# Issuing the attention scores inside the output matmuls, and re-splitting the fill's evacuations, in a fused attention and FFN kernel

## The chip, the cores and the metric

The kernel runs on one core of a Trainium2 chip. The metric is the device time of one execution in microseconds (us). A profiled execution also gives a span, which is about 1.8 us less than the time measured for the same execution. The granted clock is the share of TensorE's full speed that the profile reports; a drop is a stretch in which it reads 0.50.

## The reference, cut to what matters

For each of 64 heads (8 batches, 8 heads, 576 tokens, 64 channels) the reference adds two attentions: one over a band of 7 tokens, and one over the sequence pooled 4 to 1. The result, 4608 tokens of 512 channels, goes through a gated FFN.

```python
out_d     = softmax(scale * q_d @ k_d.T) @ v_d           # pooled 4:1, then repeated 4 times
out_local = softmax(where(|i-j| < 4, scale * q @ k.T, -1e9)) @ v
x   = (out_up + out_local)                               # [4608, 512]
out = (relu(x @ w_gate) * (x @ w_val)) @ w_out           # d_ff = 1536
```

## The kernel before: the parts that matter

The kernel handles two heads ("a pair", `hp`) at a time. The first four pairs are done alone (the fill). Then 36 slots follow; a slot does a quarter of an FFN chunk of 512 tokens (three `h` groups of 8 matmuls, one `y` group of 12) and, up to slot 27, one pair of attention. The program is scheduled by hand: each engine gets its instructions in the order in which they are written. `ps` is the program's result buffer in PSUM, eight banks of 128x512 values. Every matmul writes into a bank, and ScalarE or VectorE has to read a result out (an evacuation) before the program writes that bank again. A dummy is a matmul on zeros, put in to keep TensorE's clock up.

```python
def emit_qkT_pe(hp, b0, b1):                # fill and slots 0 to 3: transpose and pool q, k on TensorE
    ...                                     # 24 matmuls into three PSUM banks
    nc.scalar.copy(out=big[:, 0], in_=t0[:, :, 0:96])            # bank 1 of 3
    nc.scalar.copy(out=sml[:, 0], in_=t0[:, :, 96:120])
    nc.vector.tensor_copy(out=sml[:, 1:3], in_=t1[:, :, :, 96:120])   # banks 2 and 3
    nc.vector.tensor_copy(out=big[:, 1:3], in_=t1[:, :, :, 0:96])

def emit_s1(hp, p0):                        # scores: four banks p0..p0+3, then exp and mask
    for c in range(2):                      # c=0 writes p0, p0+1; c=1 writes p0+2, p0+3
        ...
def emit_s2w(hp):                           # weighted sum into banks 4 to 7
    ...
    # ScalarE: Ln, Ln, Exp ; VectorE: two multiplies, banks 4-5 then 6-7, which frees them
def emit_fill(hp):
    emit_in(hp + 4); emit_s1(hp, 2); emit_vd(hp, 6)
    emit_warm(3)                            # dummy matmuls 128x512 on zeros
    if hp >= 1: emit_x_pe(hp - 1, 0)        # x back to channels-first; ScalarE copies it out
    if hp < LEAD - 1: emit_qkT_pe(hp + 1, 2, 3)
    else: emit_warm(3)
    emit_s2(hp, 6, 0); emit_warm(1)

def emit_slot(s, gate):                     # cut: slots above 4
    ...
    if s > 4:
        if hp < NP: emit_s1(hp, 4)          # scores in banks 4 to 7
        emit_y(c - 1, s % 4, 2)             # 12 matmuls
        ...                                 # slots 5 to 8: emit_vd
        if hp + 1 < NP: emit_pool(hp + 1)   # VectorE: reduce for the next pair's pooled scores
        emit_h(c, jj, 0)()
        if hp < NP: emit_s2w(hp)
        emit_h(c, jj + 1, 1)()
        gate = emit_h(c, jj + 2, 0)
        ...
    # slots 1 to 4: other order; slot 4 issues emit_pool(9) after its scores
...
emit_warm(15)                               # before the first pair
```

The softmax here doesn't subtract the row's maximum and nothing guards it: scores larger than these inputs give would overflow.

Of the kernel before, what the change touches and what calls it, by code (L numbers as in the profile page):

```python
# [12 lines left out]
ALU = mybir.AluOpType  # L13
# [33 lines left out]
def _sap(t_ap: bass.AP, part, extra_off: int, free_dims) -> bass.AP:  # L47
    pitch = t_ap.ap[0][0]
    lo, n = part
    return bass.AP(  # L50
        tensor=t_ap.tensor,
        offset=t_ap.offset + lo * pitch + extra_off,
        ap=[[pitch, n]] + list(free_dims),
    )
# [3 lines left out]
def kernel(  # L58
# [10 lines left out]
    nc = tc.nc  # L69
# [14 lines left out]
    NTP = 9  # L84
# [122 lines left out]
    def emit_qkT_pe(hp, b0, b1):  # L207
        r, r4, r2 = hp % NL, hp % 4, hp % 2
        sv = qk16[r].rearrange("p i (h j d) -> p i h j d", h=2, d=64)
        for n in range(2 * NB):  # L210
            lo = 120 * (n % 4)
            bank = b0 if n < 4 else b1 + n // 4 - 1
            for hh in range(2):
                nc.tensor.matmul(  # L214
                    out=ps[64 * hh : 64 * hh + 64, bank, lo : lo + 120],
                    lhsT=sv[:, n // NB, hh, n % NB, :],
                    rhs=eyesum_sb,
                    start=True,
                    stop=True,
                )  # L220
        big = qkT[r4][:, 0 : 2 * S].rearrange("p (b n t) -> p b n t", b=3, n=4)
        sml = qkd[r2].rearrange("p i t -> p (i t)").rearrange("p (b n t) -> p b n t", b=3, n=4)
        t0 = ps[:, b0, 0:480].rearrange("p (n t) -> p n t", n=4)
        t1 = ps[:, b1 : b1 + 2, 0:480].rearrange("p b (n t) -> p b n t", n=4)
        nc.scalar.copy(out=big[:, 0], in_=t0[:, :, 0:96])
        nc.scalar.copy(out=sml[:, 0], in_=t0[:, :, 96:120])
        nc.vector.tensor_copy(out=sml[:, 1:3], in_=t1[:, :, :, 96:120])
        nc.vector.tensor_copy(out=big[:, 1:3], in_=t1[:, :, :, 0:96])

    def emit_vd_pool(hp):  # L230
        t, m, o = v4[hp % NV4], v2[hp % 2], vd[hp % 3]
# [65 lines left out]
    def emit_s2(hp, bank, pu):  # L297
        r2 = hp % 2
        x = xo[hp % 3]
        vflat = vw[hp % NL].rearrange("p b c -> p (b c)")  # L300
        for hh in range(2):
            for tcx in range(2):
                for c in range(2):
                    s0 = c * SD + 72 * tcx
                    lo = 130 * hh + 65 * tcx
                    nc.tensor.matmul(
                        out=ps[:, bank, lo : lo + 65],
                        lhsT=ed[r2][:, hh, s0 : s0 + 128],
                        rhs=vd[hp % 3][:, c, 127 * hh : 127 * hh + 65],
                        start=(c == 0),  # L310
                        stop=(c == 1),
                    )
        for hh in range(2):
            for j in range(NB):
                nc.tensor.matmul(
                    out=ps[:, 2 * pu + hh, 65 * j : 65 * j + 65],
                    lhsT=ee[r2][:, hh, NQ * j : NQ * j + 128],
                    rhs=vflat[:, 128 * (NB * hh + j) - hh : 128 * (NB * hh + j) - hh + 65],
                    start=True,
                    stop=True,  # L320
                )
        rd = small.tile([72, 2, 2], FP32, name="rd", tag="rd")
        nc.vector.reciprocal(out=rd, in_=_sap(ps, (0, 72), 512 * bank + 64, [[66, 2], [65, 2]]))
        nc.vector.tensor_tensor(
            out=x[0:72, NB : NB + 2, :].rearrange("p t (h d) -> p h t d", h=2),
            in0=_sap(ps, (0, 72), 512 * bank, [[131, 2], [65, 2], [1, 64]]),
            in1=_sap(rd, (0, 72), 0, [[2, 2], [1, 2], [0, 64]]),
            op=ALU.mult,
        )
        ru = small.tile([96, 2, NB], FP32, name="ru", tag="ru")  # L330
        nc.vector.reciprocal(out=ru, in_=_sap(ps, (0, 96), 1024 * pu + 64, [[448, 2], [65, NB]]))
        nc.vector.tensor_tensor(
            out=x[:, 0:NB, :].rearrange("p j (h d) -> p h j d", h=2),
            in0=_sap(ps, (0, 96), 1024 * pu, [[513, 2], [65, NB], [1, 64]]),
            in1=_sap(ru, (0, 96), 0, [[NB, 2], [1, NB], [0, 64]]),
            op=ALU.mult,
        )

    def emit_s2t(hp, between):
        r2 = hp % 2  # L340
# [95 lines left out]
    def emit_x_pe(hp, pp):  # L436
        b, kk = hp // NPB, hp % NPB
        x = xo[hp % 3]
        for g in range(2):
            flat = pair(pp)[:, g, 0:288]  # L440
            nc.tensor.matmul(
                out=flat, lhsT=x[0:72, NB + g, :], rhs=rep4_sb, start=True, stop=False
            )
            for jj in range(3):
                nc.tensor.matmul(
                    out=flat[:, NQ * jj : NQ * jj + NQ],
                    lhsT=x[:, 3 * g + jj, :],
                    rhs=eye_sb,
                    start=False,
                    stop=(jj == 2),  # L450
                )
        o = xT[:, kk, b * S : b * S + S].rearrange("p (g t) -> p g t", g=2)
        nc.scalar.copy(out=o, in_=pair(pp)[:, :, 0:288])

    gts = {}

# [18 lines left out]

        return gate

    def emit_y(c, ty, bank):
        y_ps = ps[:, bank, :]
        for jj in range(NJJ):  # L480
            nc.tensor.matmul(  # L481
                out=y_ps,
                lhsT=gts[c, jj][:, bass.ts(ty, 128)],
                rhs=wo_sb[:, jj, :],
                start=(jj == 0),
                stop=(jj == NJJ - 1),
            )
        y_sb = ffn.tile([128, D_MODEL], FP32, name="y_sb", tag="y_sb")
        nc.scalar.copy(out=y_sb, in_=y_ps)  # L489
        r0 = c * TCH + ty * 128  # L490
        done = 0
        while done < 128:
            real = (r0 + done + B0 * S) % NTOK
            n = min(128 - done, NTOK - real)
            nc.scalar.dma_start(
                _dap(out, real * D_MODEL, [[D_MODEL, n], [1, D_MODEL]]), y_sb[done : done + n, :]
            )
            done += n
# [32 lines left out]
    def emit_fill(hp):  # L531
        emit_in(hp + 4)
        emit_s1(hp, 2)
        emit_vd(hp, 6)
        emit_warm(3)
        if hp >= 1:
            emit_x_pe(hp - 1, 0)
        if hp < LEAD - 1:
            emit_qkT_pe(hp + 1, 2, 3)
        else:  # L540
            emit_warm(3)
        emit_s2(hp, 6, 0)
        emit_warm(1)

    def emit_slot(s, gate):
        c, jj, hp = s // 4, 3 * (s % 4), s + LEAD
        if NVP <= hp + 1 < NP:
            emit_vd_pool(hp + 1)
        emit_in(hp + 4)
        if NTP <= hp + 3 < NP:  # L550
            emit_qkT(hp + 3)
        if s == 0:
            emit_qkT_pe(hp, 2, 3)
            emit_warm(2)
            emit_x_pe(hp - 1, 0)
            emit_warm(1)
        elif s <= 5:
            emit_s2t(hp - 1, gate)
        elif gate:
            gate()  # L560
        if s > 4:
            if hp < NP:
                emit_s1(hp, 4)
            emit_y(c - 1, s % 4, 2)
            if hp < NVP:
                emit_vd(hp, 3)
            if hp + 1 < NP:
                emit_pool(hp + 1)
            emit_h(c, jj, 0)()
            if hp < NP:  # L570
                emit_s2w(hp)
            emit_h(c, jj + 1, 1)()
            gate = emit_h(c, jj + 2, 0)
            if hp < NP:
                gate()
                emit_xsum(hp)
                return None
            return gate
        if s == 4:
            emit_y(c - 1, s % 4, 1)  # L580
        else:
            emit_h(c, jj, 0)()
        emit_s1(hp, 4)
        if NTP <= hp + 1:
            emit_pool(hp + 1)
        if s == 4:
            emit_h(c, jj, 0)()
        emit_h(c, jj + 1, 1)()
        emit_vd(hp, 5)
        if hp + 1 < NTP:  # L590
            emit_qkT_pe(hp + 1, 4, 0)
        return emit_h(c, jj + 2, 3)

    with tc.manual_schedule(engines={ET.PE, ET.DVE, ET.Activation, ET.SP, ET.Pool}):
        nc.sync.dma_start(cst_sb, cst_dr)
        for hp in range(4):
            emit_in(hp)
        emit_warm(15)
        emit_qkT_pe(0, 2, 3)
        for hp in range(LEAD):  # L600
            emit_fill(hp)
        gate = None
        for s in range(NCH * 4):
            gate = emit_slot(s, gate)
        gate()
        for ty in range(4):
            emit_y(NCH - 1, ty, ty)
# [30 lines left out]
```

## Time and profile before

| | before |
|---|---|
| time, median of the three runs given | 373.0 us (373.0 to 374.79) |
| span of the profiled execution (time 374.69) | 372.8 us |
| TensorE busy | 96% of the span |
| steady slot, slots 9 to 27 (slots 6 to 8, with emit_vd, take 9.89) | 9.55 us |
| one pair of the fill | 4.47 us |

The page's first part gives each engine's busy time, its share of the span and its instructions; PEld is the weight load.

```profile
span 372.8 us, 7223 instructions
PE 357.8 (96%) x2871; PEld 181.1 (49%) x2871; DVE 228.9 (61%) x332; ACT 211.5 (57%) x355; POOL 177.9 (48%) x219
```

The 96% does not say that TensorE is the limit. The chain of waits does better: it lists, in order of time, what the end of the program hung on. Start, duration and engine of one steady slot of the kernel before (the query lists the longest pieces; the weighted sum, before Ln, and the scores, before y, are left out):

```profile
135.05 2.70 PE ps L481 x12
137.74 1.73 PE ps L461 x8
139.90 0.77 ACT rden_113 L423
140.69 0.77 ACT rden_113 L423
141.48 0.81 ACT rden_113 L426
142.36 0.89 issue
143.25 0.92 DVE xn_115 L429
144.60 2.70 PE ps L481 x12
```

L481 is y, L461 is h, L423 and L426 are Ln and Exp, L429 the multiply. "issue" covers the first of the two multiplies. The period is one loop through three engines, and for about 4 us of it, from Ln to the second multiply, TensorE does h work that is not on the loop. The timeline of the same slot shows where the loop touches TensorE (start, duration, engine, operation; in brackets the idle time before it and what ended that):

```profile
142.32 1.84 DVE L429 TENSOR_TENSOR xn_115<-ps,rden_113 64x720 f16<-64x720 f32 x2 [2.06 <-ACT rden_113 L426]
142.68 1.03 PE L461 MATMUL ps<-xT,wv_sb 128*128 128x512 f16 x4
143.64 0.25 PE L261 MATMUL ps<-qkd_100 64*72 64x144 f16 x2
144.22 0.25 PE L261 MATMUL ps<-qkd_100 64*72 64x144 f16 x2 [0.20 <-DVE xn_115 L429]
144.53 2.76 PE L481 MATMUL ps<-wo_sb,gT 128*128 128x512 f16 x12
```

The first half of the scores (L261 and its band part) starts at 143.64. The second half writes banks 6 and 7 and waits until the second multiply has read them, at 144.16. From the end of h, about 143.54, to y at 144.53 is 0.99 us; the same scores without a wait, in slot 0, took 0.59.

In the fill the same reading gives another engine. VectorE's copy of two banks ends last, and the next scores wait for it:

```profile
17.39 0.95 DVE L228 CAST qkT_98<-ps 128x768 f16<-128x768 f32 x1
18.39 0.22 PE L261 MATMUL ps<-qkd_100 64*72 64x144 f16 x1 [0.27 <-DVE qkT_98 L228]
```

Slot 5 is a place of its own. The table of stretches gives the stretch, its length, the busy time of PE, PEld, DVE, ACT and POOL with their instructions, the granted TensorE clock, and the DMA share and GB/s:

```profile
71.00:74.60 3.60, 2.00 (x49) 1.59 (x49) 1.59 (x2) 2.90 (x5) 3.60 (x5) 1.00 2.14 179
74.60:79.00 4.40, 4.36 (x14) 1.69 (x14) 2.76 (x4) 0.69 (x2) 3.05 (x5) 0.61 2.01 138
```

TensorE stood still several times before 74.6 us, and then its clock fell; y took 4.44 us there instead of 2.70.

### The profile page before, as it was taken

What the parts mean: (1) busy time and instruction counts of PE and PEld (TensorE: products, weight loads), DVE (VectorE), ACT (ScalarE), POOL (GpSimd) and SP (SyncE); (2) the same over time, 40 slices, a digit from 0 to 9 for tenths busy, and PEclk for the clock granted to TensorE, in tenths of its full rate; (3) what the DMA queues carried; (4) which work ended last, traced back from release to release, by engine and by line L of the source; (5) the groups of instructions that cost most, each with busy time, mean ns of one, the idle gap of its engine ahead of it and who ended that gap; (6) DMA issues with size and microseconds to landing.
All of it is one profiled execution on the core that took longest, in us unless ns stands there. A gap on an engine that the chain in (4) does not pass through costs nothing.

```text
span 372.8 us, 7223 instructions
## 1 busy us (share of the span) xinstructions
PE 357.8 (96%) x2871; PEld 181.1 (49%) x2871; DVE 228.9 (61%) x332; ACT 211.5 (57%) x355; POOL 177.9 (48%) x219
## 2 busy tenths in 40 slices
PE   7899999899999999999999999999999999999995
PEld 3665555445554444444444444444444544444442
DVE  8674566538777877777777667776666522222220
ACT  2664775646666666666666666666666533332321
POOL 8966548757667776777777777621000000000000
PEclk9999999989999999999999999999999999999999
DMA  9999999999999999999999999961000001000012
GB/s 129 169 173 184 177 196 124 169 134 175 180 107 115 118 132 113 132 123 111 127 128 122 125 122 125 120 100 48 28 31 28 30 28 56 31 28 30 28 56 84
DMA packets 165137, 39.51 MB, mean 106 GB/s; under 512 B 149264, under 2 KB 160368, under 8 KB 165104
## 3 DMA queue, kind: packets, MB, share of 16 engines
q0 software_dynamic: 132528, 22.48, 81.8%
q1 hardware_dynamic: 27376, 7.14, 15.0%
q10 hardware_dynamic: 5200, 9.44, 7.3%
q8 instruction: 22, 0.36, 0.4%
q14 instruction: 11, 0.09, 0.1%
HBM read 45.28 MB, written 9.44 MB: 147 GB/s over the span
## 4 chain that ended last, share of the span: by engine, by line
PE 65%; ACT 17%; DVE 10%; issue 7%; DVEq 0%
PE ps L461 29%; PE ps L481 26%; ACT rden_112 L423 5%; ACT rden_113 L423 5%; DVE xn_115 L429 3%; DVE xn_114 L429 3%; ACT rden_113 L426 2%; ACT rden_112 L426 2%; PE ps L261 2%; PE ps L405 2%; PE ps L214 1%; PE ps L245 1%; PE ps L272 1%; PE ps L413 1%; DVE xn_114 L383 1%
## 5 line engine op out<-in xcount | busy, mean ns | idle before, releaser
L461 PE MATMUL ps<-xT,wg_sb 128*128 128x512 f16 x432 | 111.0, 379 | 1.3 <-DVE xn_114 L383 0.5
L461 PE MATMUL ps<-xT,wv_sb 128*128 128x512 f16 x432 | 110.9, 379 | 0.0
L481 PE MATMUL ps<-wo_sb,gT 128*128 128x512 f16 x432 | 100.5, 384 | 0.6 <-DVE xn_114 L383 0.6
L461 PEld LDWEIGHTS <-wv_sb 128*128 128x128 f16 x432 | 42.3, 98 | 51.0
L481 PEld LDWEIGHTS <-gT 128*128 128x128 f16 x432 | 40.8, 99 | 48.9 <-issue 2.9
L461 PEld LDWEIGHTS <-wg_sb 128*128 128x128 f16 x432 | 39.7, 97 | 43.8 <-issue 1.5
L489 ACT COPY y_sb<-ps 128x512 f32<-128x512 f32 x36 | 21.1, 587 | 69.8 <-PE ps L481 69.8
L429 DVE TENSOR_TENSOR xn_115<-ps,rden_113 64x720 f16<-64x720 f32 x24 | 21.7, 905 | 24.7 <-ACT rden_113 L426 24.3
L429 DVE TENSOR_TENSOR xn_114<-ps,rden_112 64x720 f16<-64x720 f32 x22 | 19.9, 905 | 22.8 <-ACT rden_112 L426 22.4
L281 ACT ACTIVATE ee_102<-ps 112x576 f16<-112x576 f32 x32 | 19.5, 650 | 10.6 <-PE ps L272 10.0
L281 ACT ACTIVATE ee_103<-ps 112x576 f16<-112x576 f32 x32 | 19.5, 650 | 9.4 <-PE ps L272 9.2
L284 DVE TENSOR_TENSOR ee_102<-ee_102,cst_sb 112x576 f16<-112x576 f16 x32 | 21.1, 691 | 2.7 <-ACT ee_102 L281 2.5
L423 ACT ACTIVATE rden_113<-ps 64x720 f32<-64x720 f32 x24 | 18.4, 765 | 6.6 <-PE ps L413 6.3
L423 ACT ACTIVATE rden_112<-ps 64x720 f32<-64x720 f32 x22 | 16.8, 765 | 6.0 <-PE ps L413 5.8
L284 DVE TENSOR_TENSOR ee_103<-ee_103,cst_sb 112x576 f16<-112x576 f16 x32 | 19.8, 659 | 0.0
L527 PE MATMUL ps<-zero_sb 128*128 128x512 f16 x37 | 12.5, 463 | 1.3 <-DVE zero_sb L130 1.3
L261 PE MATMUL ps<-qkd_101 64*72 64x144 f16 x64 | 8.5, 244 | 3.8 <-DVE xn_114 L429 2.2
L261 PE MATMUL ps<-qkd_100 64*72 64x144 f16 x64 | 8.2, 245 | 3.8 <-DVE xn_115 L429 2.2
L388 DVE TENSOR_TENSOR xT<-xn_115 128x576 f16<-128x576 f16 x14 | 11.2, 798 | 0.1
L388 DVE TENSOR_TENSOR xT<-xn_114 128x576 f16<-128x576 f16 x14 | 10.5, 753 | 0.1
L290 ACT ACTIVATE ed_104<-ps 72x576 f16<-72x576 f32 x16 | 10.2, 639 | 0.0
L290 ACT ACTIVATE ed_105<-ps 72x576 f16<-72x576 f32 x16 | 10.2, 638 | 0.0
(457 smaller groups left out, 589.5 us busy)
## 6 DMA issues: line engine op xcount, KB each, us to landing
out_dram<-y_sb ACTq DMA_DIRECT2D x35, 256.0 KB, 3.3
wg_sb<-in_moe_w_gate_dram POOLq DMA_DIRECT2D x4, 384.0 KB, 10.0
wv_sb<-in_moe_w_val_dram POOLq DMA_DIRECT2D x4, 384.0 KB, 10.3
wo_sb<-in_moe_w_out_dram POOLq DMA_DIRECT2D x4, 384.0 KB, 11.7
vw_90<-in_v_dram POOLq DMA_DIRECT2D x5, 168.0 KB, 5.8
vw_91<-in_v_dram POOLq DMA_DIRECT2D x5, 168.0 KB, 5.4
vw_92<-in_v_dram POOLq DMA_DIRECT2D x5, 168.0 KB, 6.2
vw_89<-in_v_dram POOLq DMA_DIRECT2D x4, 168.0 KB, 8.0
```

The costliest lines, as they stand in the source:

```text
L261: nc.tensor.matmul(out=ps[0:72, p0 + 2 * c + hh, 288:432], lhsT=qkd[r2][lo : lo + 64, 1, bass.ts(c, 72)], rhs=qkd[r2][lo : lo + 64, 0, :], ...
L281: nc.scalar.activation(out=o, in_=ps[0:WK, p0 + 2 * g : p0 + 2 * g + 2, 0:288], func=AF.Exp, scale=scale)
L284: nc.vector.tensor_tensor(out=o, in0=o, in1=_sap(masks_sb, (0, WK), 288 * g, [[0, 2], [1, 288]]), op=ALU.mult,)
L290: nc.scalar.activation(out=ed[r2][:, :, 0 : 2 * SD].rearrange("p h (c t) -> p c h t", c=2), in_=ps[0:72, p0 : p0 + 4, 288:432].rearrange(" ...
L388: nc.vector.tensor_tensor(out=xT[:, kk, b * S : (b + 1) * S].rearrange("p (c t f) -> p c t f", c=2, f=4), in0=x[:, :, 0:288].rearrange("p ...
L423: nc.scalar.activation(out=r[lo : lo + 64], in_=ps[de : de + 64, 4 + 2 * hh : 6 + 2 * hh, 0:360], func=AF.Ln)
L426: nc.scalar.activation(out=r, in_=r, func=AF.Exp, scale=-1.0)
L429: nc.vector.tensor_tensor(out=x[lo : lo + 64], in0=ps[lo : lo + 64, 4 + 2 * hh : 6 + 2 * hh, 0:360], in1=r[lo : lo + 64], op=ALU.mult,)
L461: nc.tensor.matmul(out=h, lhsT=w[:, kk, bass.ts(jj, 128)], rhs=xT[:, kk, c * TCH : (c + 1) * TCH], start=(kk == 0), stop=(kk == 3),)
L481: nc.tensor.matmul(out=y_ps, lhsT=gts[c, jj][:, bass.ts(ty, 128)], rhs=wo_sb[:, jj, :], start=(jj == 0), stop=(jj == NJJ - 1),)
L489: nc.scalar.copy(out=y_sb, in_=y_ps)
L527: nc.tensor.matmul(out=ps[:, 7, :], lhsT=zero_sb[:, 0:128], rhs=zero_sb[:, 128:640], start=True, stop=True)
```

## The change

The intent is to keep TensorE working while the last multiply frees its banks. Scores are issued after two of y's matmuls; slot 5 has a form of its own. In the fill, two of the three banks go to ScalarE, the x copy goes to VectorE, the last pair's norm and copy are halved so that h can start earlier, and nine dummies are dropped. The pooling reduce for pair 9 moves from slot 4 to slot 5.

```diff
@@ emit_qkT_pe
-        nc.scalar.copy(out=big[:, 0], in_=t0[:, :, 0:96])
-        nc.scalar.copy(out=sml[:, 0], in_=t0[:, :, 96:120])
-        nc.vector.tensor_copy(out=sml[:, 1:3], in_=t1[:, :, :, 96:120])
-        nc.vector.tensor_copy(out=big[:, 1:3], in_=t1[:, :, :, 0:96])
+        for i, bank in enumerate((b0, b1, b1 + 1)):
+            t = ps[:, bank, 0:480].rearrange("p (n t) -> p n t", n=4)
+            if i < 2:
+                nc.scalar.copy(out=big[:, i], in_=t[:, :, 0:96])
+                nc.scalar.copy(out=sml[:, i], in_=t[:, :, 96:120])
+            else:
+                nc.vector.tensor_copy(out=sml[:, i], in_=t[:, :, 96:120])
+                nc.vector.tensor_copy(out=big[:, i], in_=t[:, :, 0:96])
@@ emit_s2: for the last pair of the fill the norm in two halves, (0,3) and (3,6)    ... (cut)
@@ emit_x_pe
-        nc.scalar.copy(out=o, in_=pair(pp)[:, :, 0:288])
+        if hp == LEAD - 1:
+            nc.scalar.copy(out=o[:, 0], in_=ps[:, 2 * pp, 0:288])
+            nc.vector.tensor_copy(out=o[:, 1], in_=ps[:, 2 * pp + 1, 0:288])
+        else:
+            nc.vector.tensor_copy(out=o, in_=pair(pp)[:, :, 0:288])
@@ emit_y
-    def emit_y(c, ty, bank):
+    def emit_y(c, ty, bank, cut=0, inner=None):
         for jj in range(NJJ):
+            if inner and jj == cut:
+                inner()
@@ emit_fill
-        emit_warm(3)
+        emit_warm(2)
@@ emit_slot
             emit_s2t(hp - 1, gate)
+            if s == 5:
+                emit_pool(hp)
...
             if hp < NP:
-                emit_s1(hp, 4)
-            emit_y(c - 1, s % 4, 2)
+                emit_y(c - 1, s % 4, 1 if s == 5 else 2, 6 if s == 5 else 2, lambda: emit_s1(hp, 4))
+            else:
+                emit_y(c - 1, s % 4, 2)
...
-        if NTP <= hp + 1:
-            emit_pool(hp + 1)
@@ start
-        emit_warm(15)
+        emit_warm(10)
```

More of the change, by code (lines that the diff above doesn't have):

```diff
@@ L222, in emit_qkT_pe @@
         sml = qkd[r2].rearrange("p i t -> p (i t)").rearrange("p (b n t) -> p b n t", b=3, n=4)
-        t0 = ps[:, b0, 0:480].rearrange("p (n t) -> p n t", n=4)
-        t1 = ps[:, b1 : b1 + 2, 0:480].rearrange("p b (n t) -> p b n t", n=4)
-        nc.scalar.copy(out=big[:, 0], in_=t0[:, :, 0:96])
-        nc.scalar.copy(out=sml[:, 0], in_=t0[:, :, 96:120])
-        nc.vector.tensor_copy(out=sml[:, 1:3], in_=t1[:, :, :, 96:120])
-        nc.vector.tensor_copy(out=big[:, 1:3], in_=t1[:, :, :, 0:96])
+        for i, bank in enumerate((b0, b1, b1 + 1)):
[6 more added lines that the diff above has]
+                nc.vector.tensor_copy(out=big[:, i], in_=t[:, :, 0:96])
     def emit_vd_pool(hp):
@@ L331, in emit_s2 @@
         nc.vector.reciprocal(out=ru, in_=_sap(ps, (0, 96), 1024 * pu + 64, [[448, 2], [65, NB]]))
-        nc.vector.tensor_tensor(
-            out=x[:, 0:NB, :].rearrange("p j (h d) -> p h j d", h=2),
-            in0=_sap(ps, (0, 96), 1024 * pu, [[513, 2], [65, NB], [1, 64]]),
-            in1=_sap(ru, (0, 96), 0, [[NB, 2], [1, NB], [0, 64]]),
-            op=ALU.mult,
-        )
+        for j0, j1 in ((0, 3), (3, 6)) if hp == LEAD - 1 else ((0, 6),):
+            nc.vector.tensor_tensor(
+                out=x[:, j0:j1, :].rearrange("p j (h d) -> p h j d", h=2),
+                in0=_sap(ps, (0, 96), 1024 * pu + 65 * j0, [[513, 2], [65, j1 - j0], [1, 64]]),
+                in1=_sap(ru, (0, 96), j0, [[NB, 2], [1, j1 - j0], [0, 64]]),
+                op=ALU.mult,
+            )
     def emit_s2t(hp, between):
```

## The prediction

> **What bounds it now.** TensorE is busy 96% of the span (busy table). From 296 us on (timeline) it has no wait and the change touches nothing. Before that:
>
> *Steady part, slots 6 to 27 (86 to 296 us).* A slot lasts 9.55 us (y, 12 matmuls of 128x512, starts at 144.53 and 154.08). The chain of waits runs Ln, Exp, two normalising multiplies on VectorE, second half of the scores, y, h, weighted sum. In the timeline the scores start at 143.64, their second half waits until 144.21 for the last multiply to free its banks, y starts at 144.53. From end of h (143.54) to y is 0.99 us; without the wait (slot 0, 31.14 to 31.73) the same scores cost 0.59. The stall is 0.40 us, in 22 slots (waits table: 11 + 11).
>
> *Fill (0 to 29.4 us).* A pair takes 4.47 us: scores, exp, pooled exp, transposing matmuls, evacuation; VectorE's 0.95 us copy of two banks ends last and holds the next scores (18.39).
>
> *Slot 5 (71 to 79 us).* TensorE waits several times, and the stretch table shows its clock at 0.61 from 74.6 to 79: y takes 4.44 instead of 2.70 us.
>
> **What the change does.**
>
> 1. *Scores after two y matmuls.* These take 0.43 us, so the second half would start 0.73 us after h ends; the multiply ends 0.64 after: just covered. TensorE's work per slot is then 2.59 (y) + 5.18 (h) + 0.78 (sum) + 0.59 (scores) = 9.14; the ScalarE-VectorE loop, shorter by 0.43, gives 9.12. I expect 9.15: 22 x 0.40 = **8.8 us gained**. VectorE idles 2.06 us per slot and does not take over.
>
> 2. *Fill.* VectorE keeps one bank (about 0.7 us instead of 1.25, estimated from its copies' time per element); ScalarE does two (2 x 0.62) and loses the 0.64 us x copy. ScalarE ends last; a pair takes about 4.05: three times 0.43. The first scores come 0.6 us earlier: VectorE's memsets end at 8.26 and only 0.7 follows. Halved norm and x copy before the first h: 0.3. Sum **2.1 us**. Fewer dummies save little themselves (k lands at 6.4) and may leave the clock low longer: the first run at 0.43 us each, and the Trainium skill ("TensorE: Matmul & The Clock Gate", Part 1) says about 3.4 us of sustained activity is needed for full rate. I take off 0.3.
>
> 3. *Slot 5.* y goes to another bank and six of its matmuls precede the scores. But the pooling reduce (1.35 us) that these scores need moves from slot 4, where VectorE had time, to behind the normalised sum (ends 75.38). Scores then start near 76.8, not 72.5; TensorE idles about 3.5 us, and the clock probably drops again. Scores and the other six end near 78.7 fast, 80 slow, against 78.9 before: **0.6 us lost**.
>
> **Sum.** 373.0 - 8.8 - 1.8 + 0.6 = **363.0 us**; range 360.5 to 366.0. Chances: faster 0.88, same 0.12, slower 0.0.
>
> **What would show it.** Slot period 9.15 without the scores' wait on the multiply; first h matmul at 27.3 instead of 29.4; ScalarE's evacuations ending after VectorE's; in slot 5 scores waiting about 3.5 us for the reduce; tail unchanged.
>
> **What would make it wrong.** If the scores still wait (0.07 us margin), or exp and masks, now later against y, delay the sum, the gain per slot shrinks; a clock drop in the fill loses 1 us or more; a slow restart in slot 5 could cost 1 us more. If the reduce does not hold slot 5, it gains up to 3 us.

## The result, and the profile after

The changed kernel took 365.02 us (364.98 to 365.05, 4 runs), the kernel before 373.89 us (373.0 to 375.03, 4 runs). The ratio is 0.9761, with a 95% interval of 0.9726 to 0.9796. Ratios are the mean time of one kernel's runs over the mean of the other's of the same rounds, so not quite the ratio of the medians. The forecast of 363.0 with a range of 360.5 to 366.0 holds the result; it was 2.0 us too low.

```profile
span 363.3 us, 7223 instructions
PE 351.8 (97%) x2862; PEld 179.8 (49%) x2862; DVE 226.6 (62%) x337; ACT 213.3 (59%) x370; POOL 177.4 (49%) x219
```

The chain of waits of the changed kernel, one steady slot, has no other engine left in it (L490 is y, L468 is h; the two pieces that are missing between them are the scores and the weighted sum, also on PE):

```profile
131.21 0.43 PE ps L490 x2
132.14 2.27 PE ps L490 x10
134.41 1.73 PE ps L468 x8
136.92 3.46 PE ps L468 x16
140.38 0.43 PE ps L490 x2
```

The slot is 140.38 - 131.21 = 9.17 us. The timeline shows why: two y matmuls now run while the multiply ends (138.99 + 1.84 = 140.83), and neither half of the scores waits for it.

```profile
138.99 1.84 DVE L432 TENSOR_TENSOR xn_115<-ps,rden_113 64x720 f16<-64x720 f32 x2 [1.79 <-ACT rden_113 L429]
140.21 0.59 PE L490 MATMUL ps<-wo_sb,gT 128*128 128x512 f16 x2
140.74 0.25 PE L263 MATMUL ps<-qkd_100 64*72 64x144 f16 x2
140.96 0.23 PE L263 MATMUL ps<-qkd_100 64*72 64x144 f16 x2
141.24 2.33 PE L490 MATMUL ps<-wo_sb,gT 128*128 128x512 f16 x10
```

In the fill the evacuation is shorter. ScalarE's last piece and VectorE's end together, at 18.61 and 18.67, and the scores follow at once:

```profile
18.12 0.55 DVE L230 CAST qkT_98<-ps 128x384 f16<-128x384 f32 x1
18.34 0.27 ACT L227 CAST qkd_100<-ps 128x96 f16<-128x96 f32 x1
18.71 0.25 PE L263 MATMUL ps<-qkd_100 64*72 64x144 f16 x2
```

But this pair is later than in the kernel before (18.39), not earlier. The stretches of the changed kernel say why:

```profile
7.00:9.00 2.00, 0.29 (x4) 0.16 (x4) 1.91 (x16) 0.44 (x2) 2.00 (x3) 1.00 2.35 150
9.00:11.00 2.00, 1.94 (x20) 1.03 (x21) 0.88 (x3) 1.64 (x4) 2.00 (x3) 0.64 2.40 153
11.00:13.00 2.00, 1.93 (x35) 1.82 (x35) 0.39 (x3) 1.49 (x6) 2.00 (x4) 0.50 2.39 152
13.00:15.00 2.00, 2.00 (x32) 1.40 (x30) 1.93 (x5) 0.27 (x1) 2.00 (x3) 0.50 2.39 152
15.00:17.00 2.00, 2.00 (x18) 1.37 (x16) 0.96 (x3) 1.72 (x4) 2.00 (x3) 0.66 1.85 186
```

From about 9.5 to 16.4 us TensorE ran at half clock. The kernel before had 1.00 in all these stretches, and more TensorE work in the first of them:

```profile
7.00:9.00 2.00, 1.23 (x27) 0.78 (x26) 1.90 (x16) 0.62 (x2) 2.00 (x3) 1.00 2.34 149
```

In slot 5 it is the other way round: the clock stays, though TensorE waits for the reduce, as forecast.

```profile
74.70 1.34 DVE L200 TENSOR_REDUCE qkd_101<-qkT_97 128x288 f16<-128x1152 f16 x1
76.10 0.25 PE L263 MATMUL ps<-qkd_101 64*72 64x144 f16 x2 [3.25 <-DVE qkd_101 L200]
76.60 1.47 PE L490 MATMUL ps<-wo_sb,gT 128*128 128x512 f16 x6
```

The difference of the two profiled spans, 9.5 us, splits at two points of the chain of waits: where the first h starts, and where the first h of slot 5 starts. In the kernel before:

```profile
29.41 1.89 PE ps L461 x8
79.42 1.73 PE ps L461 x8
```

In the changed kernel:

```profile
28.81 1.89 PE ps L468 x8
78.41 1.73 PE ps L468 x8
```

The same numbers are given for every run; the last column says where the granted clock dropped in that profiled execution.

| profiled execution | first h at | to first h of slot 5 | rest | span | clock drops |
|---|---|---|---|---|---|
| before | 29.41 | 50.01 | 293.4 | 372.8 | slot 5 |
| changed | 28.81 | 49.60 | 284.9 | 363.3 | fill, twice as long |
| e1 scores only | 29.39 | 50.01 | 284.8 | 364.2 | slot 5 |
| e2 dummies back | 26.89 | 50.90 | 284.8 | 362.6 | slot 5 |
| e3 reduce back | 27.58 | 46.41 | 284.8 | 358.8 | fill |
| e4 both back | 26.89 | 46.41 | 284.8 | 358.1 | none |
| e5 few dummies | 30.09 | 48.32 | 293.4 | 371.8 | fill |
| e6 one y first | 26.88 | 46.40 | 288.6 | 361.9 | none |
| e7 six y first | 26.88 | 46.40 | 284.8 | 358.1 | none |
| e8 15, then 2 per pair | 26.88 | 46.40 | 284.8 | 358.1 | none |
| e9 no halves | 27.30 | 46.40 | 284.9 | 358.6 | none |
| e10 10, then 3 per pair | 26.90 | 46.40 | 284.9 | 358.2 | none |
| e11 dummies moved | 26.90 | 46.40 | 284.9 | 358.2 | none |
| e12 slot 5 only | 29.40 | 51.19 | 293.4 | 374.0 | slot 5 |

So of the 9.5 us, 0.6 came in the fill, 0.4 up to slot 5, and 8.5 after it.

### The profile page after: what moved, and what is told of

It is laid out like the page before. It is cut to its first block, busy times and chain, and to the rows that moved or that the text cites. A ratio compares the mean times of both kernels' runs of the same rounds, so it can differ in the third digit from the quotient of the medians. Undisturbed runs are those within 1.5% of the kernel's fastest.

```text
span 363.3 us, 7223 instructions
## 1 busy us (share of the span) xinstructions
PE 351.8 (97%) x2862; PEld 179.8 (49%) x2862; DVE 226.6 (62%) x337; ACT 213.3 (59%) x370; POOL 177.4 (49%) x219
## 4 chain that ended last, share of the span: by engine, by line
PE 91%; DVE 5%; ACT 2%; issue 1%; DVEq 0%
PE ps L468 50%; PE ps L490 26%; PE ps L408 3%; PE ps L274 2%; PE ps L214 2%; PE ps L263 2%; PE ps L416 2%; PE ps L247 1%; PE ps L536 1%; DVE xn_114 L386 1%; ACT rden_112 L385 1%; ACT rden_112 L383 1%; PE ps L317 1%; PE ps L347 1%; PE ps L308 0%
## 5 line engine op out<-in xcount | busy, mean ns | idle before, releaser
L468 PE MATMUL ps<-xT,wg_sb 128*128 128x512 f16 x432 | 111.0, 379 | 0.8 <-DVE xn_114 L386 0.5
L468 PE MATMUL ps<-xT,wv_sb 128*128 128x512 f16 x432 | 110.9, 379 | 0.0
L490 PE MATMUL ps<-wo_sb,gT 128*128 128x512 f16 x432 | 102.7, 380 | 0.0
L468 PEld LDWEIGHTS <-wv_sb 128*128 128x128 f16 x432 | 42.2, 98 | 51.1
L490 PEld LDWEIGHTS <-gT 128*128 128x128 f16 x432 | 40.1, 98 | 47.0
L468 PEld LDWEIGHTS <-wg_sb 128*128 128x128 f16 x432 | 39.6, 97 | 43.4 <-issue 1.0
L283 ACT ACTIVATE ee_103<-ps 112x576 f16<-112x576 f32 x32 | 19.1, 648 | 17.1 <-PE ps L274 17.0
L283 ACT ACTIVATE ee_102<-ps 112x576 f16<-112x576 f32 x32 | 19.1, 648 | 14.7 <-PE ps L274 14.2
L286 DVE TENSOR_TENSOR ee_102<-ee_102,cst_sb 112x576 f16<-112x576 f16 x32 | 21.8, 712 | 2.7 <-ACT ee_102 L283 2.4
L286 DVE TENSOR_TENSOR ee_103<-ee_103,cst_sb 112x576 f16<-112x576 f16 x32 | 20.0, 659 | 1.7 <-ACT ee_103 L283 1.5
L536 PE MATMUL ps<-zero_sb 128*128 128x512 f16 x28 | 11.2, 512 | 1.3 <-DVE zero_sb L130 1.3
L263 PE MATMUL ps<-qkd_101 64*72 64x144 f16 x64 | 7.3, 242 | 3.2 <-DVE qkd_101 L200 3.2
L429 ACT ACTIVATE rden_113<-rden_113 128x720 f32<-128x720 f32 x12 | 9.6, 803 | 0.4
```

Source lines behind the costliest of these rows:

```text
L263: nc.tensor.matmul(out=ps[0:72, p0 + 2 * c + hh, 288:432], lhsT=qkd[r2][lo : lo + 64, 1, bass.ts(c, 72)], rhs=qkd[r2][lo : lo + 64, 0, :], ...
L283: nc.scalar.activation(out=o, in_=ps[0:WK, p0 + 2 * g : p0 + 2 * g + 2, 0:288], func=AF.Exp, scale=scale)
L286: nc.vector.tensor_tensor(out=o, in0=o, in1=_sap(masks_sb, (0, WK), 288 * g, [[0, 2], [1, 288]]), op=ALU.mult,)
L468: nc.tensor.matmul(out=h, lhsT=w[:, kk, bass.ts(jj, 128)], rhs=xT[:, kk, c * TCH : (c + 1) * TCH], start=(kk == 0), stop=(kk == 3),)
L490: nc.tensor.matmul(out=y_ps, lhsT=gts[c, jj][:, bass.ts(ty, 128)], rhs=wo_sb[:, jj, :], start=(jj == 0), stop=(jj == NJJ - 1),)
L536: nc.tensor.matmul(out=ps[:, 7, :], lhsT=zero_sb[:, 0:128], rhs=zero_sb[:, 128:640], start=True, stop=True)
```

## The experiments

My theory after the result had three parts: the whole steady gain is the covered wait; the fill's gain was eaten by a clock drop that the missing dummies let happen; the moved reduce costs time in slot 5. The rivals are in the expectations.

### e1: the scores alone

```diff
+ kernel before, with emit_y(c, ty, bank, cut, inner) and, for s > 5 only:
+     emit_y(c - 1, s % 4, 2, 2, lambda: emit_s1(hp, 4))
```

> The kernel before, with only the scores put after two y matmuls, in slots 6 to 27; fill and slot 5 as before. Theory: this alone gives the steady gain, a slot of 9.16 us in place of 9.55, 22 x 0.39 = 8.5 us; time about 364.5 us in executions whose slot 5 stays at full clock, 366.3 where it drops. Rival: the steady gain needs ScalarE or VectorE work that the other parts moved; then the slot stays above 9.3 us and the time above 368.

Measured: 366.13 us (365.91 to 366.13, 4 runs) against 374.40 (372.96 to 374.95) for the kernel before, ratio 0.9786 (0.9758 to 0.9813). The slot is 9.16 us and everything up to slot 5 is as before. The part of the span after slot 5 fell by 8.6 us, to the changed kernel's 284.8. The steady gain needs nothing else from the change.

### e2: the dummies back

```diff
- emit_warm(10)   # start          - emit_warm(2)   # per pair
+ emit_warm(15)                    + emit_warm(3)
```

> The changed kernel with its dummies put back (15 at the start, 3 per pair of the fill). Theory: the fill missed its forecast because TensorE ran at half clock until about 16.4 us; with the dummies the half clock ends near 6.5 us, the first h matmul starts near 27.4 instead of 28.8 us and the time falls by about 1.4 us to 363.6. Rival: the evacuation through ScalarE is itself slower than forecast (it takes 0.50 and 0.27 us for a bank) and dummies cost time; then the first h matmul stays at 28.8 or later.

Measured: 364.83 us (364.42 to 365.01). The fill behaved better than expected: no clock drop there, first h at 26.89. But the time fell by only 0.2 us, because in this kernel the clock dropped in slot 5: the profile has 0.50 from about 73.6 to 77.0 us, and slot 5's first h comes 1.3 us later after the start of h than in the changed kernel. So the forecast of the time was a miss, although the mechanism in the fill was as said. None of the fourteen profiles has a drop in both places, but what ties the two together, if anything does, no run shows.

### e3: the reduce back in slot 4

```diff
-            if s == 5:
-                emit_pool(hp)
+        if NTP <= hp + 1:          # slots up to 4, after the scores
+            emit_pool(hp + 1)
```

> The changed kernel with the pooling reduce of pair 9 back in slot 4, the dummies as changed. Theory: TensorE's 3.25 us wait on that reduce in slot 5 is real loss on the critical path; without it the scores follow the six y matmuls with at most 0.4 us of waiting, h of slot 5 starts about 3.1 us earlier, and the time is about 362.0. Rival: the wait only hides another (gate of slot 4, normalised sum, y bank), which takes its place; then less than 1 us is gained.

Measured: 361.86 us (360.64 to 362.61, 4 runs). From first h to slot 5's h takes 46.41 us in place of 49.60: 3.2 us gained, as the wait on the reduce said. The clock still dropped in all four executions (granted clock 0.984 to 0.994). In the profiled one it dropped in the fill and came back at 12.9 us instead of 16.4. That the four times spread because the drop lasts differently is likely, but only this one was profiled.

### e4: both back

> The changed kernel with dummies and reduce both back. If the two losses are separate they add: about 1.4 + 3.1 us, time near 360.5. If the same time were counted twice, about 362.

Measured: 359.92 us (359.91 to 360.33), ratio to the kernel before 0.9624 (0.9596 to 0.9651). The granted clock is 1.0 in all four executions. The losses add: 1.92 us earlier at the first h (26.89 against 28.81), 3.19 less up to slot 5, 5.1 in sum, and the median fell by 5.1. The first h:

```profile
26.89 1.02 PE L468 MATMUL ps<-xT,wg_sb 128*128 128x512 f16 x4
```

### e5: only fewer dummies, on the kernel before

> The kernel before with only the dummies reduced (10 at the start, 2 per pair). Theory: this part of the change alone makes the clock drop in the fill (near 9.4 us, for 3.4 or 6.9 us) and delays the first h from 29.4 to 30.5 or later; time at least 374 in executions that would otherwise take 373.0. Rival: the drop in the changed kernel came from the new evacuation, which leaves TensorE less work at that time; then the clock stays and the time too (373.0 and 374.7).

Measured: 374.24 us (373.66 to 374.59) against 372.99 (372.96 to 374.70). The profile shows the drop (0.69, 0.50 and 0.95 in the stretches 9 to 11, 11 to 13 and 13 to 15), and the first h at 30.09 instead of 29.41. One of these stretches:

```profile
11.00:13.00 2.00, 2.00 (x27) 1.18 (x24) 0.55 (x2) 1.47 (x5) 2.00 (x4) 0.50 2.39 152
```

The delay, 0.7 us, is less than I wrote (30.5 or later). The drop was shorter, 3.4 us against 6.8 in the changed kernel; e3, with the new fill and a drop of 3.4 us, also lost 0.7 (27.58 against 26.89). The drop is made by the missing dummies alone; the new evacuation is not needed for it. The ratio, 1.001 (0.998 to 1.004), is not clear of 1, since the kernel before mixes its two groups of times (373.0 and about 374.7). The granted clock, 0.989 to 0.995 in the four executions, says only that each had a drop somewhere.

### e6 and e7: how much of y goes first

On e4, with the scores after one, and after six, of y's matmuls.

```diff
- 6 if s == 5 else 2
+ 6 if s == 5 else 1          # e6
+ 6                           # e7
```

> The kernel with both put back, but in slots 6 to 27 the scores come after one y matmul in place of two. Theory: the gain is the cover of the wait on the normalising multiply, nothing else. One y matmul covers 0.22 us less, and 0.13 to 0.15 us of the wait should reappear before the second half of the scores: slot 9.29 to 9.31 us, time about 359.9 + 22 x 0.14 = 363.0. Rival: any break in the order (y first) gives the whole gain; then the slot stays at 9.16 and the time at 359.9.

> The same with the scores after six y matmuls in slots 6 to 27. Theory: TensorE's own work (9.14 us) is now the bound, so more cover gives nothing: slot 9.16, time 359.9, within 0.3. Rival: later scores push the exp and the masks into the weighted sum's start (masks end about 0.6 us before it with two y matmuls) and the slot grows by 0.2 us or more, time above 364.

Measured: e6 363.70 us (363.62 to 363.90), e7 359.95 (359.93 to 360.14). With one y matmul the second half of the scores is held back again:

```profile
136.41 0.25 PE L263 MATMUL ps<-qkd 64*72 64x144 f16 x2
136.50 0.29 PE L274 MATMUL ps<-qkT 64*128 64x96 f16 x6
136.77 0.25 PE L263 MATMUL ps<-qkd 64*72 64x144 f16 x2
137.09 2.55 PE L490 MATMUL ps<-wo_sb,gT 128*128 128x512 f16 x11
146.42 0.82 PE L490 MATMUL ps<-wo_sb,gT 128*128 128x512 f16 x3
```

The halves start 0.36 us apart instead of 0.22, and the slot is 146.42 - 137.09 = 9.33 us (the last line is the next slot's eleven matmuls, cut off by the window). The time is 0.7 us above the 363.0 that I wrote: the wait that came back is 0.17 us per slot ((288.6 - 284.8) / 22), not 0.14. The size of the gain follows the cover: none 9.55, one matmul 9.33, two 9.16, six 9.16. Past two it is flat, as TensorE's own work is then the bound; nor did later scores delay the weighted sum.

### e8, e10, e11: which dummies

All three have the reduce back in slot 4. e8: 15 at the start, 2 per pair. e10: 10 at the start, 3 per pair. e11: 3 per pair, and the 15 split around the first transposing matmuls:

```diff
-        emit_warm(15)
+        emit_warm(10)
         emit_qkT_pe(0, 2, 3)
+        emit_warm(5)
```

> Reduce back in slot 4; 15 dummies at the start, but 2 (not 3) per pair of the fill. Theory: the five dummies taken at the start are what let the clock drop at 9.4 us (TensorE is then busy 0.3 of the 2 us before 9); the one per pair is harmless. Then the first h matmul is at 26.9 and the time 359.9, clock 1.0. Rival: the dummy per pair matters as well; then the clock drops in the fill, and the first h comes at 27.5 or later.

> Reduce back; 10 dummies at the start, 3 per pair. Theory: the start dummies alone decide; the clock drops in the fill although the pairs have their 3 dummies, first h at 27.5 to 28.9, time 360.6 to 362.6 (as with both reduced). Rival: 3 per pair would have kept it, then 359.9.

> Both back, but 5 of the 15 dummies stand after the first transposing matmuls in place of before them. Same number of dummies. Theory: what counts is how long TensorE is idle between 5.5 and 9 us, not where its work sits; with the 5 dummies in the idle stretch the clock stays, first h within 0.4 us of 26.9, time 359.9 to 360.3. Rival: an unbroken run of dummies from 1.3 to 6.6 us is what keeps it; then the clock drops and the time is 360.6 or more.

Measured: e8 359.91 us (359.90 to 359.92), e11 359.93 (359.92 to 359.96), e10 362.10 with single times of 359.93, 360.88, 363.31 and 363.36. With 15 at the start the dummy per pair does not matter. The five at the start do, and it does not matter on which side of the first transposing matmuls they stand. With ten and 3 per pair, the drop comes and goes: one of the four executions kept its clock (1.0 granted, and the profile happens to be of this one), two lost more of it than the changed kernel (0.986 against 0.991). With ten and 2 per pair (changed, e3, e5) all twelve executions had a drop somewhere, so that the dummy per pair matters when ten stand at the start is not ruled out. My range of 360.6 to 362.6 for e10 was too narrow on both sides.

### e9: the halves undone

> Both put back; the last pair's norm and x copy whole again, the copy on ScalarE. The prediction gave the halves 0.3 us. The trace of the kernel with both back shows the first x matmul at 25.99, after both halves and after two dummies, so the halved norm is worth nothing there and only the split copy counts: 0.1 to 0.2 us, time 360.0 to 360.2.

Measured: 360.34 us (360.33 to 360.51), so the halves are worth 0.4 us, more than the 0.1 to 0.2 that I wrote, and close to the prediction's 0.3. The profile of e9 shows what I had overlooked:

```profile
26.62 0.64 ACT L457 CAST xT<-ps 128x576 f16<-128x576 f32 x1 [0.40 <-PE ps L448]
27.30 1.02 PE L467 MATMUL ps<-xT,wg_sb 128*128 128x512 f16 x4 [0.51 <-ACT xT L457]
```

The first h group writes the first of the two banks that x is copied from. With the copy whole, h waits for all of it; with the copy split, h starts when ScalarE has read that one bank (copy from 26.44 to 26.84, h at 26.89 in e4). The halved norm itself gives nothing: in e4 the x matmuls start at 25.99, after both halves and after two dummies that end then, and in e9 at 25.91. This last point is read from the traces; the norm was not undone alone.

### e12: slot 5 alone, on the kernel before

> The kernel before with only slot 5 changed (six y matmuls before the scores, y to another bank, reduce moved). Theory: it costs about 1.3 us against executions of the kernel before whose slot 5 ran at full clock (373.0) and gains 0.3 against those where it dropped (374.7): time 374.3 where the clock stays, 375.6 where it drops. Rival: the move of the reduce frees VectorE in slot 4 and is worth something there; then below 373.0.

Measured: 375.87 us (375.80 to 377.18, 4 runs) against 372.99 (372.96 to 374.70), ratio 1.0064 (1.0031 to 1.0097). The slot-5 part of the change is a loss by itself:

```profile
76.69 0.34 PE L261 MATMUL ps<-qkd 64*72 64x144 f16 x2 [3.25 <-DVE qkd L200]
77.56 2.70 PE L483 MATMUL ps<-wo_sb,gT 128*128 128x512 f16 x6
```

TensorE waits 3.25 us for the reduce, and then six matmuls take 2.70 us, at half clock. The loss is 1.2 us against the profiled execution of the kernel before (51.19 - 50.01), whose clock dropped too. The rival, a use for VectorE's freed time in slot 4, fell.

### A version that beats both

e4, e7, e8 and e11 all take about 359.9 us. e8 is the changed kernel with 15 dummies at the start and the reduce in slot 4: ratio to the kernel before 0.9615 (0.9594 to 0.9635).

## Why the prediction was right, and where its sizes were off

The prediction held: faster, and inside the range. The three terms (steady, fill, slot 5) were too hopeful by 0.3, 1.2 and 0.7 us; among the three, no error hid another. Inside slot 5 one did, and that was luck: the base of the sum (point 4) made the forecast 1.7 us too hopeful, but the clock, which was expected to drop, did not. In e2 and e12, where it did, slot 5's first h came 1.3 and 1.6 us later after the start of h than in the changed kernel. With both drops the time would have been 366.3 us or more (an estimate: 365.0 + 1.3), outside the range. Point by point:

1. **Scores after two y matmuls.** Right. Predicted slot 9.15, measured 9.16 to 9.17; predicted gain 8.8 us, measured 8.5 (the table's rest, 293.4 to 284.9). e1 shows it alone, e6 and e7 show that it is the cover of the wait, and that two matmuls are just enough, as the margin of 0.07 us had said. TensorE's own work in a slot was estimated at 9.14 us; y's 12 matmuls at 2.59 us, or 0.216 each, agree with the 215.7 ns that the Trainium skill ("TensorE: Matmul & The Clock Gate", "Wait — 56ns, not 53.3ns?") gives for a warm stream of 512 columns.

2. **Fill.** The mechanism was right and the term for the clock was mis-sized. Evacuation, pair period and halves together were put at 2.1 us. With the clock kept (e4) they give 29.41 - 26.89 = 2.5 us; a pair takes 3.97 us (18.71 to 22.68 in the changed kernel, after its drop) rather than 4.05. ScalarE was to end last; the two engines' copies in fact end within 0.06 us of each other (18.61 and 18.67). For the dummies I took off 0.3 us. They cost 1.9 us (28.81 - 26.89). I had also named the wrong form, "leave the clock low longer": the first scores, at 8.69 us, ran as fast as later ones (0.25 us for two matmuls, as at 18.71; at half clock, in e12, 0.34), and then came a drop of 6.8 us, after the stretch 7 to 9 us in which TensorE had 0.29 us of work. The same page of the Trainium skill, in its section "Part 1: The HAM clock gate", gives a free-running window of 3413 ns; the drops of these runs, worked out from short stretches, last 3.4 us (before, 74.74 to 78.16; as long in e1, e2, e3, e5 and e12) and 6.8 us (changed, 9.54 to 16.37), one and two such windows, which agrees.

3. **Slot 5.** Right that the moved reduce holds the scores and that this loses time: scores forecast to wait about 3.5 us, measured 3.25; the clock was forecast to drop, and in the changed kernel's profile it did not. In e2 and e12, with the same code for slot 5, it did. The prediction's two ends, 78.7 us with the clock kept and 80 with a drop, against 78.9, mean 0.2 us gained or 1.1 lost; against the profiled execution of the kernel before, the changed kernel gained 0.4 and e12 lost 1.2. The 0.6 lost in the sum lies between the two cases.

4. **The base of the sum.** This is the step that I did not see. I read slot 5 from a profiled execution that took 374.69 us, with a clock drop in it, and subtracted from 373.0 us, the time of executions without it. In the 21 timed executions of the kernel before in the three rounds of experiments, 8 took 373.0 us with a granted clock of 0.998 or more, and 13 took 374.4 to 375.0 with 0.995 or less. e5's profile shows the old slot 5 without the drop: 48.32 us from first h to slot 5's h, 1.7 less than 50.01. Against those executions the changed slot 5 loses 49.60 - 48.32 = 1.3 us. The sum then closes: 373.0 - 8.5 - 0.6 + 1.3 = 365.2, measured 365.0.

What stays open is why the clock stays in one execution and drops in the next of the same kernel, and what share of work in a window is enough. The executions show both outcomes with the same code (the kernel before, and e10); the start of the window against the kernel would do it, but no run controls that.

## What to carry to other kernels

When an engine waits at a fixed place in a loop for another engine to free a buffer, put independent work of its own there, as much as the wait is long: here 0.43 us of y covered 0.40 us of waiting in each of 22 slots. Half of that cover left part of the wait, and six matmuls instead of two gave nothing further and did no harm. Before you take dummy matmuls out, look at the granted clock in the stretch that follows, not at the time that the dummies take; leaving out nine cost 1.9 us here, through the five at the start. And do not add a term read from one profiled execution to a median of others before you have checked that both belong to the same group of times.

## What the Trainium skill lacked or had wrong

- "TensorE: Matmul & The Clock Gate", "Why this matters for your kernels", advises no idle gaps of TensorE above about 3 us. That was not enough here. The changed kernel's clock dropped at 9.54 us although the longest gap before it was 1.75 us (TensorE busy 1.51 of the last 3.41 us), and the kernel before dropped in slot 5 with no gap above 0.6 us (busy 1.76 of the 3.41 us up to 74.74). The same gap of 3.25 us in slot 5 came without a drop in the changed kernel and with one in e2 and e12. The page also says that frequent short idles between groups of matmuls make the clock oscillate, but it gives no figure for how much work a partly busy window needs. The records of busy time are modelled, so no threshold is read from this.
- The same page, Part 1, puts the cost of the first cold stretch under 1% and advises against modelling it. It says that the number of cold matmuls varies from run to run. It does not say that the dummies at the start decide about a later drop, worth 1.9 of 365 us here, nor that a single-core kernel's times fall into groups through such drops: the kernel before has two, 373.0 and about 374.7 us, and e10 ranges from 359.9 to 363.4.
- The same page, "Back-to-back issue gap", gives about 131 ns per matmul for a sustained stream of weight loads and matmuls at 512 columns, and calls the 216 ns of the isolated formula too long. Here the sustained stream runs at 216 ns: in the part without attention (kernel before, chain of waits) 36 matmuls with their loads take 7.77 us, from y at 296.52 to y at 304.29.
- The granted clock of the profile reads 1.00 from 0 to 7 us, while the dummies start 0.43 us apart, which is the page's cold spacing (426.7 ns). The page warns in general that clock events in a trace can be unreliable; no page says that the first, cold stretch can be missing from this column.
